# Reordering the start and the crossbar queue of a fused attention and feed-forward kernel

## The chip, the cores and the metric

The kernel runs on one core of a Trainium2 chip. The time is the device time of one execution in microseconds; several executions are made and the median is used. TensorE multiplies matrices (and transposes by multiplying with an identity), VectorE, ScalarE and GpSimd (POOL) do elementwise work, and SyncE (SP) issues transfers. POOL issues the loads of the inputs, and SyncE issues the stores and the transposes that the DMA engines' crossbar does. Each engine works through its own instructions in order and waits on semaphores.

## The reference

For 8 batches and 8 heads with 576 positions of 64 elements, 32 packed rows p per head attend to k and v, and then q attends to the 32 packed results. The output, read as 4608 tokens of 512, goes through a feed-forward layer whose activation is h cos(h).

```python
def _attn_ref(q, k, v, p):
    scale = 1.0 / np.sqrt(q.shape[-1])
    def sm_attn(qq, kk, vv):
        s = scale * np.matmul(qq, kk.transpose(0, 1, 3, 2))
        s = s - np.max(s, axis=-1, keepdims=True)
        a = np.exp(s)
        a = a / (np.sum(a, axis=-1, keepdims=True) + 1e-09)
        return np.matmul(a, vv)
    p_packed = sm_attn(p, k, v)
    return sm_attn(q, p_packed, p_packed)

def _moe_ref(x, w_in, w_out):
    h = x @ w_in          # 4608 x 512 by 512 x 2048
    g = h * np.cos(h)
    return g @ w_out      # 4608 x 2048 by 2048 x 512
```

## The kernel before

The work goes batch by batch, and everything is held in bf16 with sums in float32. For one batch b these steps follow one another.

`load` brings k, q or v of the batch from memory with a cast to bf16, issued by POOL. k has two buffers, q and v have one each. `permute_v` rearranges v into `vp` (by VectorE for batch 0, by POOL for the others). q and k have to be transposed: batch 0's q and k and batch 1's by TensorE (`pe_T`), the later ones by the crossbar (`xbar`, issued by SyncE). `s1` computes the scores of p against k (L128) and ScalarE takes their exponentials into `a1` (L137). a1 is transposed into `a1T`, by TensorE in `a1_pe` (L161, batches 0 to 2) or by the crossbar in `a1_xbar` (L151, from batch 3 on). `pp` multiplies a1T with vp (L169), and four small copies write the result into `ppT`; two go to the first engine of its `engs`, two to the second. `ppw` multiplies ppT with a quarter of w_in (L193) into `PPW`, so that the feed-forward's first product is folded into the packed values. `s2` computes the scores of q against ppT and its exponentials `a2u`; `sums2` and `normalise` divide by their sums, giving `a2n` (L229).

Then come 16 h steps (`h_mm`): four matmuls of PPW and a2n (L242), the cosine by ScalarE (L246) and the product by VectorE into `gT` (L249). After every eight of them POOL copies the last 64 columns of each gT row block into `joint` (L253). The second product, gT with w_out (L295), is cut into single matmuls that a generator hands out (`fill`); those of batch b - 1 are put between the steps of batch b, so that TensorE has work while the others finish. Finished chunks are copied to `osb` and stored by SyncE (L302).

The order on every engine is the order of the program text, since the schedule is manual. `slot` deals out the fills over the 16 h steps of a batch and calls hooks after given steps: in the loop for s = 3 to 7, `pp(s + 1)` after h step 5 and two quarters of `ppw` after step 10. `warm` runs matmuls without use, to keep TensorE busy at the start.

PSUM has two pools: psA, three buffers of two banks each (`psa`), used in turn by scores, transposes, pp, ppw and h steps, and psO, two banks (`bank`), for the second product and, in batch 0, for ppw and other steps called with `own`.

The loads are held back by gates: a one-element POOL copy reads the result of a crossbar transpose, so that POOL issues the next loads, or whatever stands behind them, only after that transpose has landed. In the steady loop the SyncE order is q of batch s + 1, k of batch s + 2, a1 of batch s + 1, and the gate reads a1T:

```python
            xbar("q", s + 1)
            if s + 2 < B:
                xbar("k", s + 2)
            a1_xbar(s + 1)
            recips(s + 1)
            G.tensor_copy(out=gate, in_=a1T[s + 1][0:1, 0, 0, 0:1])
```

Of the kernel before, what the change touches and what calls it, by code (L numbers as in the profile page):

```python
# [15 lines left out]
def kernel(  # L16
# [64 lines left out]
    def load(n, b):  # L81
        bf[n, b] = bf_pool.tile([TP, H, C * D], BF16, name=n + "bf", tag=n + "bf", bufs=2 if n == "k" else 1)
        G.dma_start(out=bf[n, b], in_=srcs[n][b].rearrange("h (p c) d -> p h (c d)", c=C))
# [10 lines left out]
    def pe_T(n, b, engs=(V, V, V), groups=(0, 1, 2), own=False):  # L94
        if 0 in groups:
            xT[n, b] = att_pool.tile([128, H * 3, TP], BF16, name=n + "T", tag=n + "T", bufs=2 if n == "k" else 1)
        t = xT[n, b]
        flat = bf[n, b].rearrange("p h x -> p (h x)")
        for i in groups:
            ps = bank(BF16) if own else psa(BF16)[:, 0, :]  # L100
            for j in range(8):
                o = 8 * i + j
                nc.tensor.transpose(ps[:, j * TP:(j + 1) * TP], flat[:, o * 128:(o + 1) * 128],
                                    ident[0:TP, 0:TP])
            copy(engs[i], t[:, 8 * i:8 * i + 8].rearrange("p a x -> p (a x)"),
                 ps[:, 0:8 * TP])

    def bank(dt=FP32):
        return O.tile([128, 512 if dt == FP32 else 1024], dt, name="ot", tag="ot")

    def pack_p(b0, b1, flat=None):
        ng = 2 * (b1 - b0)
        if flat is None:
            flat = psa(BF16).rearrange("p a x -> p (a x)")
        for g in range(ng):
            nc.tensor.transpose(flat[:, g * 128:(g + 1) * 128],
                                p_bf[:, 2 * b0 + g].rearrange("p t d -> p (t d)"), ident)
        V.tensor_copy(out=P2[:, b0:b1].rearrange("p b h n -> p (b h n)"), in_=flat[:, 0:ng * 128])
# [14 lines left out]
    def s1(b):  # L133
        ps = scores(P2[:, b], xT["k", b])
        sm = small.tile([128, 2], FP32, name="sums1")
        for y in range(2):
            ACT.activation(  # L137
                out=a1[b % 2][:, y, :, 0:TP].rearrange("p (e m) x -> p e m x", e=2),
                in_=ps[y][:, :, 0:HS].rearrange("p e (m x) -> p e m x", m=3),
                func=AF.Exp, scale=scale, accum_out=sm[:, y:y + 1])  # L140
        sums1[b] = sm

    def recips(b):
        r1[b] = small.tile([128, 2], FP32, name="r1")
        rs1[b] = small.tile([128, 2], FP32, name="rs1")
        V.reciprocal(r1[b], sums1[b])
        V.tensor_scalar(out=rs1[b], in0=r1[b], scalar1=scale, scalar2=None, op0=ALU.mult)  # L147
# [6 lines left out]
    def a1_pe(b, ys=(0, 1), own=False):  # L154
        if 0 in ys:
            a1T[b] = att_pool.tile([128, 2, C, 128], BF16, name="a1T", tag="a1T")
        t = a1T[b]
        for y in ys:
            ps = bank(BF16) if own else psa(BF16)[:, 0, :]
            for c in range(C):  # L160
                nc.tensor.transpose(ps[0:TP, c * 128:(c + 1) * 128], a1[b % 2][:, y, c, 0:TP], ident)  # L161
            copy(V, t[0:TP, y].rearrange("p c x -> p (c x)"), ps[0:TP, 0:C * 128])

    def pp(b, own=False, engs=(V, ACT)):
        ps = bank() if own else psa()[:, 0, :]
        for hp in range(4):
            for j in range(C):
                c = 2 * (j % 3) + j // 3
                nc.tensor.matmul(ps[:, hp * 64:(hp + 1) * 64], vp[b][:, c, hp * 128:(hp + 1) * 128],  # L169
                                 a1T[b][0:TP, :, j, 32 * hp:32 * hp + 32], start=(j == 0), stop=(j == C - 1))  # L170
        pv = ps[:, 0:256].rearrange("p (a y x) -> p a y x", a=4, y=2)
        t = ppT[b % 2].rearrange("p (a y) x -> p a y x", y=2)
        for y in range(2):
            r = slice(64 * y, 64 * y + 64)
            copy(engs[0], t[r, :, y, :], pv[r, :, y, :])
        for y in range(2):
            r = slice(64 * y, 64 * y + 64)
            z = slice(64 - 64 * y, 128 - 64 * y)
            copy(engs[1], t[z, :, y, :], pv[r, :, y, :])

    def ppw(b, n, eng=None, own=False, later=False, cuts=((0, 512),)):
        if b not in PPW:
            PPW[b] = ppw_pool.tile([128, 2, DF], BF16, name="PPW", tag="PPW")
        two = isinstance(eng, tuple)
        if own:
            ps = [bank(), bank()]
        else:
            t = psa()
            ps = [t[:, 0, :], t[:, 1, :]]
        for x in range(4):  # L190
            for y in range(2):
                r = slice(64 * y, 64 * y + 64)
                nc.tensor.matmul(ps[y][32 * x:32 * x + 32, :], ppT[b % 2][r, 2 * x + y, :],  # L193
                                 w_in_bf[r, x, n * 512:(n + 1) * 512], start=True, stop=True)

        def evacuate():
            if own or two:
                for a, z in cuts:
                    for y in range(2):
                        copy(eng[y] if two else eng, PPW[b][:, y, n * 512 + a:n * 512 + z], ps[y][:, a:z])  # L200
            else:
                copy(eng or (V, ACT)[n % 2], PPW[b][:, :, n * 512:(n + 1) * 512], t)
        if later:
            return evacuate
        evacuate()

    def s2(b):
        a2u[b] = att_pool.tile([128, 2, S], BF16, name="a2u", tag="a2u")
        ps = scores(ppT[b % 2], xT["q", b])
        for y in range(2):  # L210
            ACT.activation(out=a2u[b][:, y].rearrange("p (e x) -> p e x", e=2),  # L211
                           in_=ps[y][:, :, 0:HS], func=AF.Exp, scale=rs1[b][:, y:y + 1])
# [113 lines left out]
    def dup_p(a, b, eng):  # L326
        for t in range(2):
            eng.tensor_copy(out=p_bf[:, a:b, t, :], in_=p_raw[:, a:b, :])

    def warm(n):  # L330
        wps = bank()
        for _ in range(n):
            nc.tensor.matmul(wps, wz[:, 0:128], wz, start=True, stop=True)
# [5 lines left out]
    load("q", 0)  # L339
    load("k", 1)  # L340
    G.dma_start(out=p_raw[:, 2:4, :], in_=p_rows[:, 2:4, :])
    for n in range(4):
        load_w_in(n)
    wz = const.tile([128, 512], BF16, name="wz")
    V.memset(wz, 0.0)
# [12 lines left out]
    s1(0)  # L358
    permute_v(0, V)
    load("v", 1)  # L360
    warm(3)
    a1_pe(0)
    warm(2)
# [5 lines left out]
        load_w_out(n)  # L369
    G.dma_start(out=p_raw[:, 4:, :], in_=p_rows[:, 4:, :])  # L370
    s2(0)
    dup_p(2, 4, V)
    pack_p(1, 2, bank(BF16))
    warm(2)
    sums2(0, 0)
    sums2(0, 1)
    pe_T("k", 1, (V, V, V))
    warm(2)
    first_ppw = ppw(0, 0, V, own=True, later=True, cuts=((0, 128), (128, 512)))
    normalise(0)  # L380
    first_ppw()
    s1(1)
    recips(1)
    load("k", 2)
    permute_v(1)
    for fc in range(NFC):
        h_mm(0, fc)()
        if fc in (1, 5, 8):
            ppw(0, 1 + fc // 4, (ACT, V), own=True)
        if fc in (3, 4):  # L390
            a1_pe(1, (fc - 3,), own=True)
        if fc == 10:
            pp(1, own=True, engs=(ACT, ACT))
        if fc in (11, 12, 13):
            pe_T("q", 1, (V, ACT, V), (fc - 11,), own=True)
        if fc == 13:
            set_filler(0)
        if fc >= 14:
            fill(2)
# [71 lines left out]
    for n, b in (("v", 4), ("q", 4), ("k", 5)):  # L471
        load(n, b)
    fill(8)
    slot(2, [(3, lambda: pw2(2, 2, (ACT, V))), (7, lambda: pp(3)), (11, lambda: pw2(3))], 5, {11: 3})

    for s in range(3, B):
        nxt = s + 1 < B
        fill(1000)
        set_filler(s - 1)
        ACT.preload_act_table_set(EXP_SET)  # L480
        if nxt:
            permute_v(s + 1)
        s2(s)
        ppw(s, 2, V)
        fill(8)
        if nxt:
            s1(s + 1)
            ppw(s, 3, V)
            xbar("q", s + 1)
            if s + 2 < B:  # L490
                xbar("k", s + 2)
            a1_xbar(s + 1)
            recips(s + 1)
            G.tensor_copy(out=gate, in_=a1T[s + 1][0:1, 0, 0, 0:1])
        else:
            ppw(s, 3, V)
        fill(4)
        sums2(s, 0)
        fill(5)
        sums2(s, 1)  # L500
        normalise(s)
        fill(13)
        for n, b in (("v", s + 2), ("q", s + 2), ("k", s + 3)):
            if b < B:
                load(n, b)
        slot(s, [(5, lambda: pp(s + 1)), (10, lambda: pw2(s + 1))] if nxt else [], 5, {10: 3})
    set_filler(B - 1)
    fill(1000)
    tail_chunk(B - 1, 4)
# [30 lines left out]
```

## Time and profile before

| | |
|---|---|
| Median of 8 runs | 256.97 us (255.51 to 259.07) |
| The profiled execution's time | 259.07 us |
| Its span in the profile | 257.0 us |
| TensorE busy | 234.5 us (91%) |
| VectorE busy | 164.2 us (64%) |
| ScalarE busy | 167.9 us (65%) |
| POOL busy | 59.0 us (23%) |
| Mean granted TensorE clock | 0.993 |

The time of an execution contains about 2 us that lie outside its span. Times in the profile count from the span's start. In a timeline, a line gives the start and the length in microseconds, the engine (SPq is SyncE's issue of a transfer), the line of the kernel, the operation, what it writes and reads, how often, and in square brackets how long the engine was idle before it and what ended that. The windows give, for each stretch, its length, the busy time of TensorE, its weight loads, VectorE, ScalarE and POOL, then the granted TensorE clock as a share of full speed, and the transfers. The waits list who waited for whom: the total in microseconds, how often, and the longest.

### The profile page before, as it was taken

How to read it: one execution, taken by the hardware profiler on the slowest of the kernel's cores; microseconds unless marked ns; L12 is line 12 of the kernel's file. 1: busy time of each engine (PE TensorE's matmuls, PEld its weight loads, DVE VectorE, ACT ScalarE, POOL GpSimd, SP SyncE). 2: the span in 40 equal slices, each digit the busy share in tenths (PEclk: the TensorE clock that was granted, in tenths of full speed). 3: DMA queues.
4: the chain of work that ended last, by engine and by line, in shares of the span. 5: the costliest groups of instructions: out<-in, count | busy, mean ns of one | idle time of the engine just before them, and what ended most of it. 6: DMA issues, size and time to landing. Idle time of an engine off the chain costs nothing.

```text
span 257.0 us, 4996 instructions
## 1 busy us (share of the span) xinstructions
PE 234.5 (91%) x1980; PEld 131.7 (51%) x2013; DVE 164.2 (64%) x255; ACT 167.9 (65%) x275; POOL 59.0 (23%) x72
## 2 busy tenths in 40 slices
PE   8777778999889999969999998999999999999993
PEld 3553463566344654545545654564446554565452
DVE  2558986789476877466847774579657764776110
ACT  1369688856668587946887657777876675874000
POOL 8433424200542145013040405020510000000000
PEclk9999999999999999988999999999999999999999
DMA  6999999999899989999989993989291111112232
GB/s 94 203 211 206 205 206 220 202 166 174 162 234 187 148 165 221 224 209 161 162 127 209 157 209 85 173 157 203 66 181 43 41 43 41 46 41 57 63 82 82
DMA packets 65270, 37.67 MB, mean 147 GB/s; under 512 B 37872, under 2 KB 60656, under 8 KB 65248
## 3 DMA queue, kind: packets, MB, share of 16 engines
q0 software_dynamic: 23184, 18.81, 48.1%
q1 hardware_dynamic: 41904, 18.42, 36.5%
q8 instruction: 15, 0.25, 0.4%
q10 hardware_dynamic: 160, 0.13, 0.2%
q14 instruction: 7, 0.06, 0.1%
HBM read 37.22 MB, written 9.44 MB: 182 GB/s over the span
## 4 chain that ended last, share of the span: by engine, by line
PE 71%; DMA 12%; ACT 6%; DVE 6%; issue 2%; POOL 1%; DVEq 0%; ACTq 0%; POOLq 0%
PE ot L295 42%; PE psA L242 20%; DMA vbf<-in_v_dram 10%; DVE gT L249 4%; PE psA L193 3%; ACT cosT L246 2%; PE psA L169 2%; DMA a1T<-a 1%; PE psA L219 1%; PE ot L281 1%; ACT a2u L211 1%; POOL vp L76 1%; ACT L480 1%; PE psA L128 1%; DVE rs L147 1%
## 5 line engine op out<-in xcount | busy, mean ns | idle before, releaser
L295 PE MATMUL ot<-w_out_bf,gT 128*128 128x512 bf16 x483 | 127.3, 380 | 2.1 <-issue 1.3
L249 DVE TENSOR_TENSOR gT<-psA,cosT 128x576 bf16<-128x576 f32 x128 | 93.5, 754 | 33.2 <-ACT cosT L246 31.9
L246 ACT ACTIVATE cosT<-psA 128x576 bf16<-128x576 f32 x128 | 82.3, 652 | 27.3 <-PE psA L242 26.3
L242 PE MATMUL psA<-a2n,PPW 128*128 128x288 bf16 x512 | 84.3, 287 | 3.7 <-DVE gT L249 2.0
L295 PEld LDWEIGHTS <-gT 128*128 128x128 bf16 x512 | 48.1, 98 | 42.6 <-issue 6.1
L242 PEld LDWEIGHTS <-PPW 128*128 128x128 bf16 x512 | 49.4, 98 | 38.1 <-issue 5.6
L76 DVE CAST PPW<-psA 128x1024 bf16<-128x1024 f32 (+1 forms) x23 | 25.8, 1129 | 12.1 <-PE psA L193 12.1
L253 POOL COPY joint<-gT 128x512 bf16<-128x512 bf16 x16 | 9.8, 615 | 84.9 <-DVE gT L249 84.9
L76 DVE COPY osb<-ot 128x512 f32<-128x512 f32 (+1 forms) x19 | 12.8, 671 | 16.9 <-PE ot L295 13.8
L74 ACT COPY osb<-ot 128x512 f32<-128x512 f32 (+1 forms) x18 | 10.3, 573 | 18.7 <-PE ot L295 14.1
L76 POOL COPY vp<-vbf 96x3072 bf16<-96x3072 bf16 x7 | 19.2, 2748 | 4.9 <-DMA vbf<-in_v_dram 4.8
L229 DVE SCALAR_TENSOR_TENSOR a2n<-a2u,r,lns 128x576 bf16<-128x576 bf16 x16 | 12.4, 815 | 9.6 <-ACT lns L227 9.6
L221 ACT ACTIVATE lns<-psA 128x576 f32<-128x576 f32 x16 | 10.2, 651 | 6.2 <-PE psA L219 5.7
L137 ACT ACTIVATE a<-psA 128x576 bf16<-128x576 f32 x16 | 10.3, 649 | 4.6 <-PE psA L128 4.6
L74 ACT CAST ppT<-psA 64x128 bf16<-64x128 f32 x14 | 3.6, 260 | 13.9 <-DVE ppT L76 11.0
L295 PE MATMUL ot<-w_out_bf,joint 128*128 128x512 bf16 x46 | 12.4, 379 | 0.1
L193 PE MATMUL psA<-w_in_bf,ppT 64*32 64x512 bf16 x224 | 10.4, 381 | 1.5 <-DVE gT L249 1.1
L211 ACT ACTIVATE a2u<-psA,rs 128x576 bf16<-128x576 f32 x16 | 11.0, 738 | 1.2 <-PE psA L128 1.0
L246 ACT ACT_TABLE_LOAD x8 | 10.3, 1283 | 0.1
L169 PE MATMUL psA<-a1T,vp 96*128 96x64 bf16 x168 | 6.6, 200 | 3.9 <-DMA a1T<-a 2.3
L227 ACT ACTIVATE lns<-lns 128x576 f32<-128x576 f32 x16 | 10.0, 680 | 0.0
L169 PEld LDWEIGHTS <-vp 96*128 96x128 bf16 x192 | 7.0, 102 | 5.9 <-issue 3.2
(71 smaller groups left out, 149.0 us busy)
## 6 DMA issues: line engine op xcount, KB each, us to landing
kbf<-in_k_dram POOLq DMA_DIRECT2D x8, 576.0 KB, 12.5
vbf<-in_v_dram POOLq DMA_DIRECT2D x8, 576.0 KB, 7.5
qbf<-in_q_dram POOLq DMA_DIRECT2D x8, 576.0 KB, 9.4
out_dram<-osb SPq DMA_DIRECT2D x24, 192.0 KB, 2.6
out_dram<-osb SPq DMA_DIRECT2D x22, 128.0 KB, 2.4
w_in_bf<-in_moe_w_in_dram POOLq DMA_DIRECT2D x4, 512.0 KB, 16.5
w_out_bf<-in_moe_w_out_dram POOLq DMA_DIRECT2D x4, 512.0 KB, 20.9
out_dram<-osb SPq DMA_DIRECT2D x26, 64.0 KB, 2.0
```

What stands on the lines that cost most here:

```text
L74: ACT.copy(out=out, in_=in_)
L76: eng.tensor_copy(out=out, in_=in_)
L137: ACT.activation(out=a1[b % 2][:, y, :, 0:TP].rearrange("p (e m) x -> p e m x", e=2), in_=ps[y][:, :, 0:HS].rearrange("p e (m x) -> p e m ...
L169: nc.tensor.matmul(ps[:, hp * 64:(hp + 1) * 64], vp[b][:, c, hp * 128:(hp + 1) * 128], a1T[b][0:TP, :, j, 32 * hp:32 * hp + 32], start=(j ...
L193: nc.tensor.matmul(ps[y][32 * x:32 * x + 32, :], ppT[b % 2][r, 2 * x + y, :], w_in_bf[r, x, n * 512:(n + 1) * 512], start=True, stop=True)
L211: ACT.activation(out=a2u[b][:, y].rearrange("p (e x) -> p e x", e=2), in_=ps[y][:, :, 0:HS], func=AF.Exp, scale=rs1[b][:, y:y + 1])
L221: ACT.activation(out=lns[b][:, y].rearrange("p (e x) -> p e x", e=2), in_=ps[:, :, 0:HS], func=AF.Ln)
L229: V.scalar_tensor_tensor(out=a2n[b][:, y], in0=a2u[b][:, y], scalar=r1[b][:, y:y + 1], in1=lns[b][:, y], op0=ALU.mult, op1=ALU.mult)
L242: nc.tensor.matmul(ps[:, e, 0:HS], PPW[b][:, y, fc * 128:(fc + 1) * 128], a2n[b][:, y, e * HS:(e + 1) * HS], start=(y == 0), stop=(y == 1))
L246: ACT.activation(out=csv, in_=ps[:, :, 0:HS], func=AF.Sin, bias=PI_HALF)
L249: V.tensor_tensor(out=gT[b][:, fc, :].rearrange("p (e x) -> p e x", e=2), in0=ps[:, :, 0:HS], in1=csv, op=ALU.mult)
L295: nc.tensor.matmul(pss[c], w, w_out_bf[:, fc, :], start=(fc == 0), stop=(fc == NFC - 1))
```

## The change

It has four parts.

- In the start, the transposes of batch 1's exponentials move from the h steps of batch 0 to the place right after `s1(1)`, through a new function `a1_one` that does both halves in one psA buffer; the larger part of the PPW casts of batch 0's first quarter (`rest_ppw`) comes behind them. The transposes of batch 1's p (`pack_p(1, 2, ...)`) move behind those of its k, and the warm-up matmuls around them change.
- The load of v of batch 1 is issued ahead of the last quarter of w_in.
- In the loop from s = 3 on, SyncE issues q, a1, k instead of q, k, a1; q is issued one step earlier, ahead of `fill(8)`; the gate reads k's transpose.
- The copies of pp from batch 3 on are all done by ScalarE.

```diff
+    def a1_one(b):
+        t = a1T[b] = att_pool.tile([128, 2, C, 128], BF16, name="a1T", tag="a1T")
+        ps = psa(BF16)
+        for y in range(2):
+            for c in range(C):
+                nc.tensor.transpose(ps[0:TP, y, c * 128:(c + 1) * 128], a1[b % 2][:, y, c, 0:TP], ident)
+            copy(V, t[0:TP, y].rearrange("p c x -> p (c x)"), ps[0:TP, y, 0:C * 128])
+
...
-    for n in range(4):
+    for n in range(3):
         load_w_in(n)
...
     load("v", 1)
+    load_w_in(3)
     warm(3)
...
     s2(0)
+    warm(3)
     dup_p(2, 4, V)
-    pack_p(1, 2, bank(BF16))
-    warm(2)
     sums2(0, 0)
     sums2(0, 1)
     pe_T("k", 1, (V, V, V))
+    pack_p(1, 2, bank(BF16))
     warm(2)
-    first_ppw = ppw(0, 0, V, own=True, later=True, cuts=((0, 128), (128, 512)))
+    cut_ppw, rest_ppw = ppw(0, 0, V, own=True, later=True, cuts=((0, 128), (128, 512)))
     normalise(0)
-    first_ppw()
+    cut_ppw()
     s1(1)
+    a1_one(1)
+    rest_ppw()
     recips(1)
...
         h_mm(0, fc)()
         if fc in (1, 5, 8):
             ppw(0, 1 + fc // 4, (ACT, V), own=True)
-        if fc in (3, 4):
-            a1_pe(1, (fc - 3,), own=True)
...
-    slot(2, [(3, lambda: pw2(2, 2, (ACT, V))), (7, lambda: pp(3)), (11, lambda: pw2(3))], 5, {11: 3})
+    slot(2, [(3, lambda: pw2(2, 2, (ACT, V))), (7, lambda: pp(3, engs=(ACT, ACT))), (11, lambda: pw2(3))], 5, {11: 3})
...
         s2(s)
         ppw(s, 2, V)
+        if nxt:
+            xbar("q", s + 1)
         fill(8)
         if nxt:
             s1(s + 1)
             ppw(s, 3, V)
-            xbar("q", s + 1)
+            a1_xbar(s + 1)
+            recips(s + 1)
             if s + 2 < B:
                 xbar("k", s + 2)
-            a1_xbar(s + 1)
-            recips(s + 1)
-            G.tensor_copy(out=gate, in_=a1T[s + 1][0:1, 0, 0, 0:1])
+                G.tensor_copy(out=gate, in_=xT["k", s + 2][0:1, 0, 0:1])
...
-        slot(s, [(5, lambda: pp(s + 1)), (10, lambda: pw2(s + 1))] if nxt else [], 5, {10: 3})
+        slot(s, [(5, lambda: pp(s + 1, engs=(ACT, ACT))), (10, lambda: pw2(s + 1))] if nxt else [], 5, {10: 3})
```

## The prediction

> **What bounds the kernel now.** I read the page's busy shares first: TensorE carries 234.5 of 257.0 us, the other engines about two thirds. So nearly every microsecond to be won is one in which TensorE sits idle or runs slowly, and the next views are the granted clock (row PEclk of the page) and TensorE's waits.
>
> ```profile
> PE 234.5 (91%) x1980; PEld 131.7 (51%) x2013; DVE 164.2 (64%) x255; ACT 167.9 (65%) x275; POOL 59.0 (23%) x72
> ...
> PEclk9999999999999999988999999999999999999999
> ```
>
> ```profile
> PE psA L169 <- DMA a1T<-a: 2.3, 1, 2.3
> PE psA L242 <- DVE gT L249: 2.0, 6, 0.5
> PE psA L169 <- DVE rs L147: 1.4, 1, 1.4
> ...
> PE ot L193 <- DVE a1T L76: 1.2, 2, 0.8
> ```
>
> The longest wait is one of `pp` (L169) for a crossbar transpose of a1, and the only dip of the clock is in the same slices. The timeline of slot 3 (h steps of batch 3, 107 to 127 us) shows how it comes about:
>
> ```profile
> 102.57 4.48 SPq L92 DMA_TRANSPOSE qT<-qbf  x1
> ...
> 107.15 3.08 SPq L92 DMA_TRANSPOSE kT<-kbf  x1
> ...
> 110.32 1.51 SPq L151 DMA_TRANSPOSE a1T<-a  x1
> ...
> 114.30 1.44 PE L169 MATMUL psA<-a1T,vp 96*128 96x64 bf16 x24 [2.26 <-DMA a1T<-a]
> ```
>
> SyncE issues q, k, a1 one after another. The a1 crossbar is issued last, lands 3.84 us after its issue, and pp(4), at TensorE's head from 112.04, waits until 114.30. The same 24 matmuls take 0.87 us elsewhere and 1.44 us here, and the windows say why:
>
> ```profile
> 113.80:114.00 0.20, 0.00 (x0) 0.00 (x0) 0.00 (x0) 0.00 (x0) 0.00 (x0) 0.86 0.96 297
> 114.00:114.20 0.20, 0.00 (x0) 0.00 (x0) 0.00 (x0) 0.00 (x0) 0.00 (x0) 0.50 0.80 256
> ...
> 117.20:117.40 0.20, 0.20 (x3) 0.11 (x2) 0.00 (x0) 0.00 (x0) 0.00 (x0) 0.61 0.92 119
> ```
>
> The column after the five engines is the granted clock: 1.00 until 1.9 us into the gap, 0.50 from 113.95 to 117.35, then 1.00 again.
>
> The second wait worth a look is at 71.40. The waits put it down to a small VectorE instruction, but in the instruction order the weight load of that pp(2) waits for POOL, and the timeline shows POOL's copy `vp` (permute_v(2)) ending at 71.35, behind a gate on the crossbar of k of batch 3:
>
> ```profile
> 66.74 0.18 POOL L435 COPY gate<-kT 1x1 bf16<-1x1 bf16 x1 [18.55 <-DMA kT<-kbf]
> ...
> 68.60 2.75 POOL L76 COPY vp<-vbf 96x3072 bf16<-96x3072 bf16 x1
> ...
> 71.40 0.87 PE L169 MATMUL psA<-a1T,vp 96*128 96x64 bf16 x24 [1.44 <-DVE rs L147]
> ```
>
> That gate hangs on transfers alone. The loads run one after another from the start (one w_in quarter lands every 2.5 us), batch 2's k lands at 48.9, and three crossbars follow it (issued 48.96, 55.86, 61.71). Until 71.4 the transfers set the time, not the engines. The chain goes on behind it (q of batch 4 lands at 102.5, when its crossbar starts), but there TensorE is full: 6.45 of 6.50 us in 73.0 to 79.5.
>
> **The change part by part.**
>
> *Start, before 40 us.* Batch 1's transposes (12 matmuls, 1.0 us) leave the h steps, where they stood at 25.14 and 26.18, for TensorE's hole at 20.53 to 21.70 (1.17 us). The two a1T copies (2 x 0.544 us) move ahead of VectorE's remaining PPW casts, so the first gT comes about 0.46 us later than 23.84. In return the two waits of ppw(0,2) for a bank held by a1T (0.48 + 0.76 us) go, and VectorE, 16.05 of 18.70 us busy in 21.7 to 40.4, has 1.09 us less there. a1_one holds one of three psA buffers until about 22.8; h step 2 wants it at 23.5, so that is free. pack_p(1) behind the kT copies puts 0.29 us of VectorE before a2n (19.90); without its 0.73 us wait the row sums and their logarithms start up to 0.45 us sooner, so about nothing. Three warm-up matmuls replace two, in TensorE's idle time. v1 one place earlier in the load queue lands at about 27.6 instead of 30.15, and its POOL copy (2.74 us) ends near 31 instead of 32.95. The w_in quarter moved behind it costs POOL 0.78 us ahead of the q1 load, which waits for TensorE until 15.15 anyway, and lands at 30.15 instead of 27.44; ppw(0,3) read it at 30.75, so if everything comes 0.9 us sooner it waits 0.3. I put the gain of the stage at 0.9 us (0 to 1.5, as a loss at most 0.5). But pp(2) waits for POOL until 71.40 whatever the engines did, as the swap leaves the bytes ahead of batch 2's k unchanged. A gain here widens the 1.44 us gap, and a loss up to 1.44 us disappears in it. Taken: 0. If the gate were not in the way, the 0.9 us would count.
>
> *Crossbar order q, a1, k, q ahead of fill(8).* In slot 3, q of batch 4 still can't start before its load has landed (102.5), so its issue takes 102.57 to 107.05 again. Then a1, whose exponentials ended at 103.1, is issued at 107.15 in place of k and lands 3.84 us later, at 110.99. pp(4) wants it at 112.04, or 111.65 with the copies below: no wait, 0.66 us to spare. It starts at 111.65 rather than 114.30: 2.65 us. What is queued behind on SyncE is k (next read a slot later) and the output stores; their osb tiles are four deep and a chunk takes some 5 us, so a store may slip by many microseconds. The gate now waits for k, last as a1 was; k lands about 5 us after 108.7, near 114, as the gate did (114.28), so the loads behind it on POOL come no later. In slots 4 to 6 a1T was in time (140.87 against 141.91 in slot 4), so nothing there. The earlier q crossbar delays a1 nowhere: a1's exponentials end later than q's issue.
>
> *The clock.* Without the gap, the 3.05 us of work at 0.50 (114.30 to 117.35) take half: 1.5 us. Here the Trainium skill, "TensorE: Matmul & The Clock Gate", Part 1 (the HAM clock gate), differs: the clock drops after an idle window of about 3.4 us, and that window runs freely, so the phase decides. By that a gap of 2.26 us costs itself alone and the whole change brings 3.2 us; by the trace it costs 1.5 us more and the change brings 4.7. The half-speed stretch of 3.4 us agrees with the page, the drop after 1.9 us does not. I take the trace for the profiled execution[...].
>
> *Packed copies by ScalarE.* In slots 2 to 6 two VectorE copies (0.29 us each) become ScalarE copies (0.26 us). Today ScalarE waits for VectorE's, which stand behind queued gT products:
>
> ```profile
> 171.55 0.58 DVE L76 CAST ppT<-psA 64x128 bf16<-64x128 f32 x2
> ...
> 172.22 0.53 ACT L74 CAST ppT<-psA 64x128 bf16<-64x128 f32 x2 [1.38 <-DVE ppT L76]
> ...
> 174.27 0.65 PE L242 MATMUL psA<-a2n,PPW 128*128 128x288 bf16 x4 [0.52 <-DVE gT L249]
> ```
>
> ScalarE gives 1.05 us to four copies where it lost 1.38 + 0.53, so cosines come about 0.8 us sooner. TensorE stalls afterwards only in slot 5 (0.52) and slot 2 (0.39, counted above as 111.65). Taken: 0.52; at worst 0, at best 1.0.
>
> **Sum**: 2.65 + 1.5 + 0.52 = 4.7 us. The profiled execution had a span of 257.0 and a time of 259.07, the slowest of eight: it would become 254.4. The median, 256.97, is 2.1 us lower. The eight times fall into 255.51 to 257.04 (five) and 258.42 to 259.07 (three), a distance of about the clock term. So I don't take that term off the median: 256.97 - 2.65 - 0.52 = **253.8 us**.
>
> **The rivals.**
>
> *A. The clock drop moves to pp(2).* With the start 0.9 us faster the gap before 71.40 grows from 1.44 to about 2.3 us, above the 1.9 us after which the clock fell in slot 3. Half speed over 3 us costs 1.5 us: 255.3. Against it: the page's window, and a start that gains less.
>
> *B. The profiled slot 3 isn't typical.* The median execution is 2.1 us quicker, which is also about the wait itself. If most executions have no such wait, only the copies count: 256.97 - 0.9 = 256.1, no measurable change.
>
> *C. Slower: q's crossbar issue stretches.* In slot 2 it took 8.60 us (77.69 to 86.28) with loads in flight. If the same happens in slot 3, a1 waits behind it on SyncE until 111.3 and lands at 115.1: 0.8 us later than now, with a gap over 3 us that halves the clock in every execution: 256.97 + 0.8 + 1.5 - 0.9 = 258.4. It decides from an issue time of 7.7 us on. Against it: the same crossbar from the same start took 4.48.
>
> *D. The start's gain is kept.* If the gate comes earlier as well, pp(4) is bounded by a1T at 110.99: 0.66 us more, 253.1.
>
> **How the numbers follow.** Forecast 0.55, A 0.20, B 0.12, C 0.06, D 0.07. About 0.5%, 1.3 us, is what a measurement of this kernel tells from no change, so faster means below 255.7 and slower above 258.3. The forecast, D and most of A are faster: 0.78. B and the rest of A: 0.16. C: 0.06. The range 251.8 to 256.4 has the clock term in the median as its low end (252.3, less 0.5 for the copies' best case) and takes in A and B.
>
> **What would show it.** Right: pp(4) with no wait on a1T, the clock at 1.00 in slot 3, SyncE's a1 issue before k's near 107, no ScalarE wait on VectorE's ppT, and pp(2) still near 71.4 with a wider gap. Wrong: pp(2) well before 71, a clock dip at 71 to 75 (A), a1T landing after 112, or TensorE waits on ppT or on k's crossbar that are new.

## The result, and the profile after

| | before | after |
|---|---|---|
| Median, measured side by side | 257.60 us (32 runs, 255.51 to 263.54) | 254.38 us (11 runs, 253.58 to 255.78) |
| Ratio of the times | | 0.9888 (0.9860 to 0.9916) |
| The profiled execution | 259.07 us, span 257.0 | 253.99 us, span 251.9 |
| Mean granted clock in it | 0.993 | 0.998 |

The kernel became 3.2 us faster in the median, and 5.1 us between the two profiled executions. The forecast was 253.8 us for the median and 254.4 for the profiled execution. The medians in this document are over all executions of a kernel, while the ratios with their intervals leave out those that ran in a slower state, so the two can differ by some tenths of a microsecond.

The page after, its busy shares and the clock in 40 slices:

```profile
PE 233.4 (93%) x1981; PEld 130.7 (52%) x2014; DVE 162.4 (64%) x245; ACT 170.7 (68%) x285; POOL 58.5 (23%) x71
...
PEclk9999999999999999999999999999999999999999
```

The two slices with an 8 are gone. TensorE's busy time fell by 1.1 us although one more warm-up matmul runs: work at half speed counts as longer busy time (pp(4)'s 24 matmuls took 1.44 us at a clock of 0.50, and 0.86 us now). The list of TensorE's waits, which a wait for a crossbar used to head, now begins so:

```profile
PE psA L177 <- DVE rs L147: 1.7, 1, 1.7
```

Slot 3 of the timeline, first SyncE's queue and then pp(4) on TensorE (`pp` is L177 in this kernel, the h step L250, the second product L303):

```profile
103.08 3.81 SPq L92 DMA_TRANSPOSE qT<-qbf  x1
106.98 1.47 SPq L151 DMA_TRANSPOSE a1T<-a  x1
108.56 3.40 SPq L92 DMA_TRANSPOSE kT<-kbf  x1
```

```profile
111.08 0.86 PE L177 MATMUL psA<-a1T,vp 96*128 96x64 bf16 x24
```

The line of pp(4) has no square bracket: TensorE came to it from its work and went on. The windows of the two stretches in which it had waited and then run at half speed (the number after the five engines is the clock, and the first engine is TensorE):

```profile
112.00:114.30 2.30, 2.30 (x17) 1.55 (x16) 1.06 (x2) 2.21 (x6) 0.00 (x0) 1.00 0.96 216
114.30:117.40 3.10, 3.05 (x32) 1.53 (x32) 2.91 (x5) 2.52 (x4) 1.51 (x3) 1.00 0.40 94
```

And pp(2), which the forecast had pinned behind POOL; POOL's two lines, then VectorE's, TensorE's weight load and its matmuls:

```profile
66.33 0.18 POOL L444 COPY gate<-kT 1x1 bf16<-1x1 bf16 x1 [18.80 <-DMA kT<-kbf]
...
68.18 2.75 POOL L76 COPY vp<-vbf 96x3072 bf16<-96x3072 bf16 x1
```

```profile
69.01 1.96 DVE L147 TENSOR_SCALAR rs<-r 128x2 f32<-128x2 f32 x1
```

```profile
70.99 0.76 PEld L177 LDWEIGHTS <-vp 96*128 96x128 bf16 x24 [1.97 <-POOL vp L76]
```

```profile
70.99 0.87 PE L177 MATMUL psA<-a1T,vp 96*128 96x64 bf16 x24 [1.67 <-DVE rs L147]
```

The matmul's bracket names VectorE, the weight load's names POOL. Both end at 70.97 or 70.93, so this profile can't tell which one holds pp(2); experiments 5 and 12 do.

The stages can be compared by the start of the first matmuls of `s2`, which open a slot; slot 2 lasts from the start of s2(2) to that of s2(3), and so on. In the two profiled executions, in microseconds:

| | start of s2(2) | slot 2 | slot 3 | slot 4 | slot 5 | slot 6 |
|---|---|---|---|---|---|---|
| before | 73.50 | 25.43 | 29.15 | 28.44 | 26.46 | 29.11 |
| after | 73.09 | 24.84 | 25.51 | 28.44 | 26.03 | 29.11 |
| difference | 0.41 | 0.59 | 3.64 | 0 | 0.43 | 0 |

The differences add up to 5.07 us: all of the 5.08 between the two executions. The question for the experiments is which part of the change brought which of them, and why the medians differ by less.

### The profile page after: what moved, and what is told of

It is laid out like the page before. It is cut to its first block, busy times and chain, and to the rows that moved or that the text cites. A ratio compares the mean times of both kernels' runs of the same rounds, so it can differ in the third digit from the quotient of the medians.

```text
span 251.9 us, 4989 instructions
## 1 busy us (share of the span) xinstructions
PE 233.4 (93%) x1981; PEld 130.7 (52%) x2014; DVE 162.4 (64%) x245; ACT 170.7 (68%) x285; POOL 58.5 (23%) x71
## 4 chain that ended last, share of the span: by engine, by line
PE 74%; DVE 8%; ACT 7%; DMA 5%; issue 2%; POOL 2%; DVEq 0%; POOLq 0%; ACTq 0%
PE ot L303 42%; PE psA L250 22%; DMA w_in_bf<-in_moe_w_in_dram 5%; DVE gT L257 5%; PE psA L201 3%; ACT cosT L254 3%; PE psA L177 2%; PE psA L227 1%; PE ot L289 1%; ACT a2u L219 1%; ACT L489 1%; PE psA L128 1%; DVE osb L76 1%; DVE rs L147 1%; DVE PPW L76 1%
## 5 line engine op out<-in xcount | busy, mean ns | idle before, releaser
L303 PE MATMUL ot<-w_out_bf,gT 128*128 128x512 bf16 x483 | 126.9, 379 | 2.1 <-issue 1.3
L250 PE MATMUL psA<-a2n,PPW 128*128 128x288 bf16 x512 | 84.0, 286 | 2.5 <-DVE PPW L76 1.0
L303 PEld LDWEIGHTS <-gT 128*128 128x128 bf16 x512 | 48.0, 98 | 42.5 <-issue 6.1
L250 PEld LDWEIGHTS <-PPW 128*128 128x128 bf16 x512 | 49.1, 98 | 36.5 <-issue 3.8
L237 DVE SCALAR_TENSOR_TENSOR a2n<-a2u,r,lns 128x576 bf16<-128x576 bf16 x16 | 12.4, 813 | 9.6 <-ACT lns L235 9.6
L303 PE MATMUL ot<-w_out_bf,joint 128*128 128x512 bf16 x46 | 12.4, 379 | 0.1
L74 ACT CAST ppT<-psA 64x128 bf16<-64x128 f32 x24 | 6.2, 260 | 5.5 <-PE psA L103 2.9
L341 PE MATMUL ot<-wz 128*128 128x512 bf16 x24 | 8.1, 477 | 1.5 <-DVE wz L353 1.2
L74 ACT CAST PPW<-psA 128x1024 bf16<-128x1024 f32 (+1 forms) x9 | 7.2, 826 | 2.6 <-PE psA L201 2.6
```

Of the source, the lines that this page charges most:

```text
L74: ACT.copy(out=out, in_=in_)
L237: V.scalar_tensor_tensor(out=a2n[b][:, y], in0=a2u[b][:, y], scalar=r1[b][:, y:y + 1], in1=lns[b][:, y], op0=ALU.mult, op1=ALU.mult)
L250: nc.tensor.matmul(ps[:, e, 0:HS], PPW[b][:, y, fc * 128:(fc + 1) * 128], a2n[b][:, y, e * HS:(e + 1) * HS], start=(y == 0), stop=(y == 1))
L303: nc.tensor.matmul(pss[c], w, w_out_bf[:, fc, :], start=(fc == 0), stop=(fc == NFC - 1))
```

## The experiments

Experiments 1 to 4 shared the runs of before with median 257.48 us (35 runs), 5 to 8 those with 258.11 (17 runs), 9 to 12 those with 257.66 (17 runs).

**1. The crossbar order alone** (`order_only`): before, with q, a1, k, q ahead of `fill(8)`, and the gate on k.

```diff
         ppw(s, 2, V)
+        if nxt:
+            xbar("q", s + 1)
         fill(8)
...
-            xbar("q", s + 1)
-            if s + 2 < B:
-                xbar("k", s + 2)
             a1_xbar(s + 1)
             recips(s + 1)
-            G.tensor_copy(out=gate, in_=a1T[s + 1][0:1, 0, 0, 0:1])
+            if s + 2 < B:
+                xbar("k", s + 2)
+                G.tensor_copy(out=gate, in_=xT["k", s + 2][0:1, 0, 0:1])
```

> The kernel before with the crossbar order q, a1, k alone (q ahead of fill(8), gate on k). Theory (the time is won at pp(4) in slot 3, where a1T lands sooner): pp(4) without a wait at about 112.0, clock 1.00 in slot 3, the ScalarE waits for VectorE's ppT still there; 2.3 us faster than before, and up to 1.5 us more in executions in which the clock fell. Rival (the gain is spread over start, order and copies): under 1.5 us. Rival (the clock dip is the larger part): the fastest executions of before gain nothing, only its slow ones disappear.

Measured: 256.04 us, ratio 0.9962 (0.9924 to 0.9999). pp(4) has no wait, and slot 3 ends when the next s2 starts, here 26.10 us after the one before:

```profile
112.08 0.86 PE L169 MATMUL psA<-a1T,vp 96*128 96x64 bf16 x24
...
116.18 0.65 PE L242 MATMUL psA<-a2n,PPW 128*128 128x288 bf16 x4 [0.47 <-DVE gT L249]
...
125.05 0.44 PE L128 MATMUL psA<-qT,ppT 64*32 64x288 bf16 x16
```

The mechanism is the forecast one, but in the median it brings 1.44 us, not 2.3, and by the ratio about 1.0 (0 to 2.0). Slots 2, 4, 5 and 6 are those of before to 0.01 us. Slot 3 is 3.05 us shorter than in the profile of before: 2.26 of wait, and so about 0.8 for the clock. The timelines of the two show why it isn't more. From the start of pp(4) to the second h step behind it before takes 3.27 us and this kernel 1.84, so the half speed has cost 1.43 us by then. To the fourth h step it is 4.90 against 4.10, for there this kernel waits 0.47 us for VectorE's gT (the line at 116.18), and before doesn't wait at all.

**2. The start alone** (`start_only`): before, with `a1_one`, the moved `pack_p` and `rest_ppw`, and v1 ahead of the last w_in quarter.

```diff
     s1(1)
+    a1_one(1)
+    rest_ppw()
     recips(1)
...
     load("v", 1)
+    load_w_in(3)
...
-        if fc in (3, 4):
-            a1_pe(1, (fc - 3,), own=True)
```

> The kernel before with the new start alone (a1_one, pack_p, v1 ahead of the w_in quarter). Theory (pp(2) waits for POOL's copy behind the gate on k's crossbar, whatever the start does): gT of h step 15 about 0.6 us sooner, pp(2) at 71.0 to 71.4 after a gap of 1.7 to 2.1 us, pp(4) still released by a1T near 114, time within 0.5 us of before. Rival (the start's gain is kept): 0.6 to 0.9 us faster. Rival (the wider gap drops the clock at 71): up to 1.5 us slower, with a clock of 0.50 after 71.

Measured: 257.78 us, ratio 1.0022 (0.9986 to 1.0058): nothing. pp(2) stands 4.67 us behind the gate, as in before, and pp(4) waits for a1T:

```profile
70.81 0.87 PE L177 MATMUL psA<-a1T,vp 96*128 96x64 bf16 x24 [1.14 <-DVE rs L147]
...
113.18 0.86 PE L177 MATMUL psA<-a1T,vp 96*128 96x64 bf16 x24 [1.73 <-DMA a1T<-a]
```

This wait of 1.73 us was also followed by half speed, from about 114.2 to 117.6 us:

```profile
115.00:116.00 1.00, 1.00 (x5) 0.49 (x4) 0.00 (x0) 0.62 (x3) 1.00 (x2) 0.50 0.77 48
```

Slot 3 took 28.86 us, 2.76 more than in experiment 1: 1.73 of wait, so about 1.0 for the clock.

**3. The copies alone** (`copies_only`).

```diff
-    slot(2, [(3, lambda: pw2(2, 2, (ACT, V))), (7, lambda: pp(3)), (11, lambda: pw2(3))], 5, {11: 3})
+    slot(2, [(3, lambda: pw2(2, 2, (ACT, V))), (7, lambda: pp(3, engs=(ACT, ACT))), (11, lambda: pw2(3))], 5, {11: 3})
...
-        slot(s, [(5, lambda: pp(s + 1)), (10, lambda: pw2(s + 1))] if nxt else [], 5, {10: 3})
+        slot(s, [(5, lambda: pp(s + 1, engs=(ACT, ACT))), (10, lambda: pw2(s + 1))] if nxt else [], 5, {10: 3})
```

> The kernel before with all four copies of pp by ScalarE from batch 3 on, nothing else. Theory: the ScalarE waits on VectorE's ppT fall from 11.0 us to about 4 (batches 0 to 2 stay), TensorE's stalls of 0.39 in slot 2 and 0.52 in slot 5 go, but the first is lost again in the wait at pp(4), so 0.5 us faster. Rival (nothing, because TensorE is full): 0 to 0.2 us. Rival (ScalarE becomes late, as it holds four copies of 0.26 us in a row): new TensorE waits on psA behind pp, 0.5 us slower or more.

Measured: 257.41 us, ratio 0.9967 (0.9921 to 1.0013); by the time alone it is inconclusive. The profile says more. ScalarE's wait on VectorE's ppT fell from 11.0 to 0.2 us (4 were expected), slot 2 is 24.84 us long (0.59 less) and slot 5 is 25.81 (0.65 less). In slot 3 pp(4) still waits, and the slot ends 26.39 us after its start:

```profile
112.24 0.86 PE L169 MATMUL psA<-a1T,vp 96*128 96x64 bf16 x24 [0.91 <-DMA a1T<-a]
...
124.61 0.44 PE L128 MATMUL psA<-qT,ppT 64*32 64x288 bf16 x16
```

That is 0.88 more than after's 25.51, the wait of 0.91 without a loss of clock. So three profiled executions with the old order waited 2.26, 1.73 and 0.91 us at the same place.

**4. pp(4) later instead of a1 sooner** (`pp4_late`): before, with the hook of slot 3 behind h step 8.

```diff
-        slot(s, [(5, lambda: pp(s + 1)), (10, lambda: pw2(s + 1))] if nxt else [], 5, {10: 3})
+        slot(s, [(8 if s == 3 else 5, lambda: pp(s + 1)), (10, lambda: pw2(s + 1))] if nxt else [], 5, {10: 3})
```

> The kernel before with one number changed: pp(4) is called after h step 8 of slot 3 and not after 5, in all else the old crossbar order. a1T lands near 114.2 as before, pp(4) comes to TensorE's head near 115, so it doesn't wait. Theory (the wait at pp(4) and the clock behind it are the whole gain of the crossbar order): as fast as order_only within 0.4 us, clock 1.00. Rival (the order gains through the gate, the earlier q or the later slots): order_only is faster than this by 1 us or more.

Measured: 255.89 us, ratio 0.9953 (0.9920 to 0.9987), the same as experiment 1 (256.04), with a1T still behind k on SyncE:

```profile
109.20 1.46 SPq L151 DMA_TRANSPOSE a1T<-a  x1
```

```profile
114.08 0.86 PE L169 MATMUL psA<-a1T,vp 96*128 96x64 bf16 x24
```

Moving the consumer past the landing is worth as much as moving the transfer: slot 3 lasts 26.15 us here and 26.10 in experiment 1. The new order has no other effect that the times or these profiles show: its gain is the wait and the half speed behind it.

**5. POOL's v copy ahead of the gate** (`vp2_early`): after, with `permute_v(2)` in front of the gate on k of batch 3. Only the position in POOL's queue changes.

```diff
     xbar("k", 3)
+    permute_v(2)
     G.tensor_copy(out=gate, in_=xT["k", 3][0:1, 0, 0:1])
...
-             (8, lambda: (permute_v(2), load("v", 3), load("k", 4)))], 4)
+             (8, lambda: (load("v", 3), load("k", 4)))], 4)
```

> The changed kernel with POOL's permute_v(2) one place earlier, ahead of the gate on k of batch 3 instead of behind it. Theory (pp(2) was pinned by that copy, and the transfers set the time until a1T of batch 4 lands): pp(2) leaves 71.0 and starts at about 69.3, bounded by its a1T copies; pp(4) then comes to TensorE's head near 109.4 but a1T lands at 110 to 111, so a part of the 1.7 us comes back as a wait there: 0.3 to 1.6 us faster than the changed kernel, 253 to 254 us. Rival (pp(2) was held by VectorE's rs, as the list of waits says): pp(2) stays near 71 and the time is that of the changed kernel, 254.4. Rival (the copy [...]harms batch 1's h steps): slower by 0.5 us or more.

Measured: 256.72 us (12 runs, 252.86 to 258.69), ratio 0.9894 (0.9840 to 0.9948). In the profile the step works: pp(2) starts sooner after the same gate, without a wait, and nothing waits in slot 3 either.

```profile
66.66 0.18 POOL L445 COPY gate<-kT 1x1 bf16<-1x1 bf16 x1 [5.07 <-DMA kT<-kbf]
```

```profile
70.17 0.87 PE L177 MATMUL psA<-a1T,vp 96*128 96x64 bf16 x24
...
110.23 0.86 PE L177 MATMUL psA<-a1T,vp 96*128 96x64 bf16 x24
```

So it was POOL that held pp(2), not VectorE's small instruction. But the time doesn't keep it: 253 to 254 us were expected, the ratio stands where after's stood (0.9888), and ten of twelve executions ran at a mean clock below 0.995. In the profiled one the clock fell in the start stage, to 0.50 from 24.1 to 27.5 us. a1T lands 4.0 us after its issue at 105.85, so pp(4) had 0.4 us to spare in the profiled execution. The next two kernels ask whether a new wait there, or the next one, eats the gain.

**6. The same with pp(4) later** (`vp2_early_pp4_late`): experiment 5 and the hook of experiment 4.

> The same, and pp(4) called after h step 8 of slot 3. Theory: no wait at pp(2) nor at pp(4), so the whole 1.7 us counts: 252.7 us, 1.6 to 2.0 faster than the changed kernel. Rival (the transfers hold elsewhere, in v, q or k of a later batch): no better than vp2_early, with a new wait on a transfer.

Measured: 253.91 us (6 runs, 252.09 to 255.69), ratio 0.9846 (0.9792 to 0.9900). The profiled execution was the slowest of the six, and shows what takes the gain where it is taken:

```profile
113.11 0.86 PE L177 MATMUL psA<-a1T,vp 96*128 96x64 bf16 x24 [0.22 <-DMA a1T<-a]
...
138.35 0.86 PE L177 MATMUL psA<-a1T,vp 96*128 96x64 bf16 x24 [1.48 <-DVE gT L257]
```

q's load took 11.8 us to land here against 9.6 in experiment 5, so its crossbar began at 104.71 instead of 102.02, and a1's is queued behind it. pp(4) was late again in spite of its later place, and pp(5), one slot on, waited 1.48 us. The bracket there names VectorE, but a1's crossbar was issued at 134.29 and lands 3.9 us later, at 138.2, just before pp(5) starts. Behind pp(2) stands the chain of loads and crossbars, as the forecast had said of the stretch behind it, though there it was called covered by a full TensorE.

**7. Experiment 6 with the start of before** (`vp2_early_oldstart`): the edit is experiment 2 undone in experiment 6.

> The same as vp2_early_pp4_late with the start of the kernel before (a1 transposes in the h steps, v1 behind w_in). Theory (the new start saves 0.64 us that the gate had hidden): with the gate out of the way it counts, so this is 0.6 us slower than vp2_early_pp4_late. Rival (the start's gain is lost elsewhere before pp(2), for example in s1(2), which waits for batch 2's k): within 0.2 us.

Measured: 253.82 us (6 runs, 252.56 to 256.35), ratio 0.9848 (0.9801 to 0.9895): the same as 6, though with intervals of 0.5% on each side an effect of 0.6 us, as it was expected, would not show. Nor do the two profiles compare the starts: s2(1) begins at 39.74 here and at 39.65 there, since the first k landed later in the execution of 6 (TensorE's transposes of it start at 8.55 us there, and at 7.63 here). From s2(1) to pp(2) it is 30.65 and 30.64 us, and 30.65 and 30.66 in experiments 5 and 12: with the gate out of the way the start stage does set pp(2). s2(4) then starts 0.69 us later here (123.74 against 123.05), and that comes from a load: q took 12.4 us to land instead of 11.8, its crossbar began at 105.50 instead of 104.71, and pp(4) waited 0.81 us for a1T instead of 0.22. Even this is gone within one slot (s2(5) at 153.15 and 153.12), for pp(5) waits until the same time in both:

```profile
138.38 0.86 PE L177 MATMUL psA<-a1T,vp 96*128 96x64 bf16 x24 [0.81 <-DMA a1T<-a]
```

What comes sooner ahead of this wait is lost in it, and in these two executions that would hold for the start as well.

**8. v1's load back in its place** (`v1_back`): after, with all four w_in quarters ahead of v1.

```diff
-    for n in range(3):
+    for n in range(4):
         load_w_in(n)
...
     load("v", 1)
-    load_w_in(3)
     warm(3)
```

> The changed kernel with v1 again behind all four w_in quarters. Theory: v1 lands at 30.2 instead of 27.7, POOL's copy ends near 33.0 instead of 31.4, pp(1) starts at 33.0 instead of 32.4, and the 0.6 us disappear in the wait at pp(2): time within 0.4 us of the changed kernel. Rival (v1 early is what the start gains): pp(2) or later steps 0.6 us later, 255.0 us.

Measured: 254.88 us (6 runs, 253.90 to 255.04), ratio 0.9885 (0.9846 to 0.9923): after's ratio. The place of v1 is worth nothing that can be measured.

**9. After again** (`after_again`), unchanged, to stand beside 10 to 12.

> The changed kernel itself, on the same chip as the next three, as their reference. Expected: 254.4 us, 0.989 of before; no wait at pp(4) in slot 3, pp(2) near 71.

Measured: 254.75 us (12 runs, 253.32 to 259.45), ratio 0.9891 (0.9857 to 0.9925).

**10. After with the start of before** (`old_start`): experiment 2 undone in after.

> The changed kernel with the start of before (a1 transposes in the h steps, v1 behind w_in); crossbar order and ScalarE's copies stay. Theory (pp(2) is pinned by POOL's copy, so the start is worth nothing here): within 0.4 us of the changed kernel, pp(2) at 71.0 to 71.4. Rival (the start is a part of the gain): 0.6 us or more slower.

Measured: 254.38 us (6 runs, 253.80 to 254.87), ratio 0.9872 (0.9837 to 0.9908): no slower than after (0.9891, measured beside it). POOL's gate and pp(2) are where they always are:

```profile
67.03 0.18 POOL L443 COPY gate<-kT 1x1 bf16<-1x1 bf16 x1 [18.36 <-DMA kT<-kbf]
```

```profile
71.70 0.87 PE L177 MATMUL psA<-a1T,vp 96*128 96x64 bf16 x24 [1.16 <-DVE rs L147]
```

From gate to pp(2) it is 4.67 us here. Over before, after and experiments 1, 2, 4 and 8 to 11 this distance is 4.66 to 4.67 us, while the gate itself stands anywhere from 65.92 to 67.03. (In experiment 3 it is 5.12: there the clock had fallen in the start, and pp(2) waited neither for POOL nor for a transfer.) Slot 3 is 25.50 us long here, as in after (25.51), so the 0.6 us that slot 3 gains over experiment 1 come from the copies.

**11. a1 first** (`a1_first`): after, with a1, q, k.

```diff
         ppw(s, 2, V)
-        if nxt:
-            xbar("q", s + 1)
         fill(8)
...
             a1_xbar(s + 1)
             recips(s + 1)
+            xbar("q", s + 1)
             if s + 2 < B:
```

> The changed kernel with SyncE's order a1, q, k, all three behind s1. Theory (a1 waits for its exponentials only, which end at 102, q for a load that lands at 101 to 105, so behind q a1T depends on the loads): a1 is issued near 102 and lands near 106, 5 us ahead of pp(4); the time is that of the changed kernel, 254.4 us, as pp(4) didn't wait in it, but executions with a late load no longer wait: a narrower spread. Rival (q comes 1.6 us later and so does the gate, with new waits in slot 4): 0.5 us or more slower.

Measured: 254.59 us (6 runs, 253.68 to 255.96), ratio 0.9883 (0.9841 to 0.9924): the same as after. a1T, issued at 102.28, lands 5.1 us later, at 107.4, so it is 3.8 us early for pp(4) at 111.21. In after it was early by 0.1 (106.98 + 4.0 against 111.08). The spare time alone brings nothing, and the spread isn't narrower, as was expected (2.3 us here, 2.2 in after).

**12. a1 first and POOL's v copy ahead of the gate** (`a1_first_vp2`): the edits of 11 and 5 together.

> The same with permute_v(2) ahead of the gate on k of batch 3. Theory (both pins are gone, pp(2) and the a1T of slots 3 and 4): pp(2) near 69.5 to 70.2, no wait at pp(4) and pp(5), 1.0 to 1.7 us faster than the changed kernel: 252.7 to 253.4 us, and faster than vp2_early_pp4_late was against before (0.9846). Rival (the transfers hold it at the next place, q or k of a later batch, or a1T of batch 3 at pp(3)): no gain over the changed kernel, with a new wait there.

Measured: **252.81 us** (6 runs, 252.11 to 253.60), ratio 0.9815 (0.9778 to 0.9852). This beats before by 4.9 us and after, measured beside it, by 1.9. Five of six executions ran at a clock of 1.00. a1's crossbar no longer waits for q's load:

```profile
101.03 3.04 SPq L151 DMA_TRANSPOSE a1T<-a  x1
...
104.17 4.49 SPq L92 DMA_TRANSPOSE qT<-qbf  x1
```

```profile
69.58 0.87 PE L177 MATMUL psA<-a1T,vp 96*128 96x64 bf16 x24
...
109.95 0.86 PE L177 MATMUL psA<-a1T,vp 96*128 96x64 bf16 x24
...
135.99 0.86 PE L177 MATMUL psA<-a1T,vp 96*128 96x64 bf16 x24
```

No wait at pp(2), pp(4) or pp(5). Here a1T lands 7.7 us after its issue, beside a load in flight, and pp(4) still has 1.2 us to spare. The moved copy brings 1.8 us over experiment 11 in the median. That it pays here and not in 5 because of the margin is likely but not shown: the intervals of the two ratios overlap, and pp(4) didn't wait in the profile of 5 either.

## Why the prediction was right

**The wait at pp(4)** went as forecast: a1's crossbar at 106.98 (forecast 107.15), no wait, the clock at 1.00. The margin was smaller than the 0.66 us of the forecast, about 0.1, since a1T took 4.0 us to land where 3.84 were taken and TensorE came earlier still. Experiments 1 and 4 show that the wait, with the half speed behind it, is all of the order's gain. For the median the term was too large: 2.26 us were read from the slowest of eight executions, and experiment 1 measures 1.44 in the median and 1.0 by the ratio. Rival B, that the profiled slot isn't typical, was half right: the wait is real in every profile with the old order and pp(4) in its place, and differs between 0.9 and 2.3 us.

**The clock.** 1.5 us were forecast for it, as half of the 3.05 us of work at half speed. That much was lost at first (1.43 us by the second h step), but 0.8 us were left of it in experiment 1 and 1.0 in experiment 2, because TensorE, at full speed, runs into a wait for VectorE's gT that the half speed had hidden. The Trainium skill ("TensorE: Matmul & The Clock Gate", Part 1, the HAM clock gate) has the clock fall after an idle window of about 3.4 us that runs freely. That the window runs freely and has this length the traces show too (in the last section). That it has to be idle they don't show: no gap here was as long as 3.4 us, and the clock fell with gaps of 2.26 and 1.73 us, though not with 0.91, nor with the 1.67 before pp(2) in after. So the place of the gap in the window does decide, as the forecast had it from the page, but a gap of 2.26 us can cost clock, as it had it from the trace.

How often it fell can be read from the mean clock of every execution. A half-speed stretch of 3.4 us takes 0.7% off the mean, and the idle end of the program at most 0.4% in the profiles here, so a mean of 0.995 or more had no full stretch. Of the 69 executions of before that were measured beside the experiments, 21 reach it; of those of experiments 2 and 3, where pp(4) waits as well, 6 of 24; of those of experiments 1 and 4, where it doesn't, 16 of 24. So the clock fell in most executions of before, and more seldom without the wait. Yet it cost little there: the 32 executions of before with about one stretch (0.9885 to 0.995) have a median of 257.51 us, and the 21 without one 257.29. (The 16 with a lower mean have 260.83; what happened in them no profile shows.) To leave the term out of the median was right in size; its ground, that the eight times fall into two groups about the clock term apart, is not confirmed as the drop's doing.

**The copies** were undersized. 0.39 in slot 2 and 0.52 in slot 5 were forecast, 0.91 in all; measured are 0.59 and 0.43. The step that failed is the sentence that TensorE stalls afterwards only in slots 2 and 5. In the profile of before slot 3 hid the same stall behind the wait for a1T and the half speed. Once these were gone it appeared (the 0.47 us at 116.18 in experiment 1), and the copies saved 0.59 there too (26.10 in experiment 1 against 25.51 in after, where the stall is gone). The three together make 1.61 us. In slots 4 and 6 they bring nothing, as the table shows.

**The start** was taken as 0, and nothing was measured for it: experiments 2, 8 and 10, each to within about 1 us. The stage itself came 0.64 us sooner in the profile (s2(1) at 38.60 instead of 39.24; 0.9 was forecast), and pp(2) stayed 4.66 us behind the gate. Of the 0.41 us by which s2(2) came earlier all is the gate's own, 66.33 against 66.74, and that varies with the execution: it is 65.92 to 66.98 in the profiles with the new start and 66.16 to 67.03 in those with the old. The sentence that the 0.9 us would count with the gate out of the way holds as far as pp(2), which then follows s2(1) at 30.64 to 30.66 us in four profiles. Whether the gain lasts to the end isn't shown: experiments 6 and 7 can't tell, and for the kernel of experiment 12, which has no wait at pp(4) or pp(5), the old start was not tried.

**The sum.** For the profiled pair 4.7 us were forecast and 5.1 came: 2.26 of wait, 0.8 of clock, 1.6 of copies and 0.4 of an earlier gate, against 2.26 (2.65 with slot 2's copies counted in), 1.5, 0.9 and 0. The shares of clock and copies in slot 3 (0.8 and 0.6) hold for the order in which they are taken here, the copies last; together they make 1.38 us. For the medians 3.2 were forecast and 3.2 came, of which the parts explain 2.6 to 3.0: 1.0 to 1.4 for the order, and 1.6 for the copies, as the profiles show them; by the ratios after stands 0.7%, 1.9 us, below experiment 1. In both sums an overestimate and an underestimate cancelled, so the closeness of the total is in part luck, and no evidence for each term.

**The other rivals.** A, a clock dip at pp(2), didn't come: the gap was 1.67 us, not 2.3, and the clock stayed at 1.00. C, a stretched q issue, didn't: 3.81 us, against 7.7 needed. D, a kept start, didn't.

**What stays open.** Why experiment 5 keeps nothing of pp(2)'s gain, while 6, 7 and 12 keep some or all. Its small margin at pp(4), 0.4 us against 1.2 in 12, would fit a wait that comes in most executions, but its one profile has no such wait. What that profile does show is the drop of the clock in the start, after which s2(1) came at 39.52 us, against 38.92 in 12, and pp(2) 0.59 us later than in 12. Whether the low clocks of the other executions come from there is not known.

## What to carry to other kernels

A stage that is made faster ahead of a wait on a chain of transfers is worth nothing until that wait goes, so follow the wait to the queue it stands in and ask what sits behind a gate there that needn't: one moved POOL copy, with the crossbar order that leaves it room, was worth more (1.9 us) than the whole rework of the start (nothing that could be measured). Order a shared transfer queue by who waits first, and compute the margin at the next consumer as well as at this one. A wait read from a single profile is a sample: look at the spread of the times before counting it in the median, and ask what else was hidden behind it, since that is what appears, or can be saved, once it goes. And a loss of clock behind a gap that differs from execution to execution is to be counted as a share of the executions, which their mean clocks give.

## What the runs showed of the hardware

The clock also fell where no single gap was long, and with the same gaps it fell in one execution and not in another. What differs is the place of a grid. Six profiles have two drops of the clock, the second behind the last matmul, and these lie a whole number of steps of 3.41 us apart: 42.0 steps in before (113.94 and 257.30 us), 69.0 in experiments 1 and 3, and 41.0, 66.0 and 67.0 in experiments 2, 5 and 11. Each stretch of half speed before the last matmul lasts one step. Where the grid lies differs from execution to execution; without a drop inside the kernel it can be read from the one behind the last matmul.

With this grid laid over the 14 profiles, TensorE was busy for a share of 0.37 (before), 0.49 (experiment 2), 0.49 (5) and 0.45 (11) of the step that ended with the drop, and for 0.56 or more of every other step up to the last matmul. So a gap counts by how much of it falls into one step. With the new start TensorE has three gaps of 0.73, 0.64 and 0.62 us within four microseconds, the same to 0.01 us in all eight profiles. In experiments 5 and 11 one step takes in all three (20.70 to 24.11 and 21.03 to 24.44 us), and the clock fell at its end. In the other six the grid parts them, and it didn't. The gap of 1.67 us before pp(2) in after is parted as well, at 70.21. The share doesn't explain everything: in experiments 1 and 3 the clock fell at 17.09 us, behind steps that were busy for 0.63 and 0.67, while such steps passed elsewhere, also in before and in experiments 4, 7 and 10, which have the old start too. More than half of what TensorE did in that step of experiment 1 was transposing (1.21 of 2.16 us); whether that counts for less is not shown.

Windows of experiment 1, then one of experiment 5 and the same of experiment 6 (the clock is the number after the five engines):

```profile
16.00:18.00 2.00, 1.02 (x14) 0.52 (x6) 0.66 (x3) 1.37 (x2) 1.57 (x3) 0.77 1.21 200
18.00:20.00 2.00, 2.00 (x20) 1.65 (x19) 0.29 (x1) 1.41 (x3) 0.17 (x2) 0.50 1.25 207
```

```profile
20.00:30.00 10.00, 7.69 (x80) 4.06 (x80) 8.42 (x17) 6.95 (x13) 4.52 (x5) 0.83 1.27 205
```

```profile
20.00:30.00 10.00, 7.35 (x86) 3.77 (x82) 8.96 (x19) 7.36 (x14) 4.26 (x5) 1.00 1.27 205
```

With the old start the drop brought s2(1) to 40.16 us in experiment 1 and 40.42 in experiment 3, against 39.24 in before, and pp(2)'s wait absorbed it: 0.34 us of the wait were left in experiment 1, none in experiment 3.

A small VectorE instruction stretched while POOL copied: the 128x2 TENSOR_SCALAR `rs` took 1.96 us at 69.01 in after, beside POOL's 2.75 us copy of vp, and 0.17 us in experiment 5, where that copy ran earlier. Because it ended with that copy, the list of waits named it, and not POOL, as what pp(2) waited for.
